# Attention with a spectral mix on one core: the next unit's keys ahead of this unit's queries, loads first, PSUM pools re-dealt, transformed rows mode-innermost, seven weight buffers

## The chip, the cores and the metric

One core of one Trainium2 chip runs the whole program. The metric is device time in microseconds (us) of one execution; lower is better. Each kernel was executed several times on a chip, beside executions of the kernel before on the same chip.

## The reference, cut to what matters

```python
# q, k, v: (8 batches, 8 heads, 576 rows, 64);  w_phi: (64, 128)
def phi(x):
    proj = x @ w_phi                                  # 128 features
    proj = proj - max(abs(proj), axis=-1)             # one value per row
    return concat([exp(proj), exp(-proj)], axis=-1)   # 256 features
kv  = phi(k).T @ v ;  z = sum(phi(k), rows)
x   = (phi(q) @ kv) / (phi(q) @ z)                    # linear attention

X   = rfft(x, axis=rows)[:64]                         # 64 modes kept
Y   = X @ (w_r + 1j * w_i)                            # one 512 x 512 matrix per mode
u   = x + irfft(Y)
out = u + relu(u @ w_ch)
```

The two mode weights are 64 x 512 x 512 numbers each, in float32: 134 MB to be read from memory, converted to bfloat16 on the way.

## The kernel before: the parts that matter

The work is cut into 16 *units*: a unit `(g, bp)` is a pair of heads `g` (4 of them) and a pair of batches `bp` (4 of them). One turn of the main loop, here called a *pass*, handles one unit. Twelve of the passes also carry four *mixes*, the products of transformed rows with the mode weights of the heads before, so there are passes without mixes (the first four) and with them. (Measured from one unit to the next, as in the tables below, that gives four lengths without mixes and ten or eleven with them. The engines are named by their short names: PE multiplies matrices, ACT, DVE and POOL work element by element, SP only issues transfers here.)

PSUM, where the matmuls put their results, is dealt out by two small functions. `one` has four buffers, `two` has two larger ones, and each call takes the next buffer in turn, once its last reader is done:

```python
    ps1 = ctx.enter_context(tc.tile_pool(name="ps1", bufs=4, space=bass.MemoryType.PSUM))
    ps2 = ctx.enter_context(tc.tile_pool(name="ps2", bufs=2, space=bass.MemoryType.PSUM))
    def one(shape, dt=F32):
        return ps1.tile(shape, dt, name="one", tag="one")
    def two(shape, dt=F32):
        return ps2.tile(shape, dt, name="two", tag="two")
```

Which product uses which of them:

```python
    def transposed(src, name):                  # used for k, then for q
        for lo, hi in ((0, 5), (5, 9)):
            ptr = one([128, hi - lo, 128], BF16)          # two halves, in `one`
            for j in range(lo, hi):
                nc.tensor.transpose(ptr[:, j - lo, :], flat[:, j * 128:(j + 1) * 128], ident_b)
            nc.scalar.copy(dst[:, lo:hi, :], ptr)         # and two copies
    # ... absmax(): projects k or q, two products in `two`, the rest in `one`
    def front(st):
        kT = transposed(st["kb"], "kT")
        # ... AB = exp(+-projection of k); ee = exp(-+max); va = v * ee
        qT = transposed(st["qb"], "qT")
        # ... AQ = exp(+-projection of q), the projections in `two`; then absmax of q
    def back(st, XT):
        pk = two([128, 2, 512])                           # the k-v product, in `two`
        # ... 40 matmuls AB x va; one copy of pk to kvz
        for i in range(2):
            pn = [two([128, 2, 512]) for _ in range(2)]   # the numerator, in `two`
            # ... 16 matmuls AQ x kvz; DVE divides them; result in xs
        # ... px: the transform of xs (in `one`), copied to XT in four pieces
    # main loop
    for n, u in enumerate(units):
        front(st[u])
        # ... issue loads of unit n+2, and of mode weights (pool of 6 buffers)
        back(st.pop(u), XTs[g])
        # ... up to four mixes
    yall = pw.tile([128, B_, DMODEL], BF16, name="yall", tag="wt")  # a weight buffer
    # ... remaining mixes; 128 small transfers gather yst into yall; output stage
```

Of the kernel before, what the change touches and what calls it, by code (L numbers as in the profile page):

```python
# [12 lines left out]
I32 = mybir.dt.int32  # L13
# [15 lines left out]
def kernel(  # L29
# [27 lines left out]
    ident_f = const.tile([128, 128], F32, name="ident_f")  # L57
    make_identity(nc, ident_f)
    ident_b = const.tile([128, 128], BF16, name="ident_b")
    nc.vector.tensor_copy(ident_b, ident_f)  # L60

    w2blk = const.tile([128, 256], BF16, name="w2blk")
    nc.vector.memset(w2blk, 0.0)
    nc.gpsimd.dma_start(w2blk[0:64, 0:128], w_phi)
    nc.gpsimd.dma_start(w2blk[64:128, 128:256], w_phi)
    wchb = const.tile([128, 4, 512], BF16, name="wchb")

    CF = const.tile([128, 6, 4, 64], BF16, name="CF")
    CI = const.tile([128, 5, 128], BF16, name="CI")

    def tables():

        def sc(i):
            return yacc[:, i, 0:320].rearrange("p (c m) -> p c m", c=5)

        sp = const
        si = sp.tile([128, 5], I32, name="si")
        nc.gpsimd.iota(si[:, 0:4], [[1, 4]], base=0, channel_multiplier=4)
        nc.gpsimd.iota(si[0:64, 4:5], [[1, 1]], base=512, channel_multiplier=1)
        nc.gpsimd.iota(si[64:128, 4:5], [[1, 1]], base=512, channel_multiplier=1)  # L80
        mi = sp.tile([128, 64], I32, name="mi")
        nc.gpsimd.iota(mi, [[4, 2], [8, NO], [1, 4]], base=0, channel_multiplier=0)
        sf = sp.tile([128, 5], F32, name="sf")
        nc.vector.tensor_copy(sf, si)
        mf = sp.tile([128, 64], F32, name="mf")
        nc.vector.tensor_copy(mf, mi)
        prodf = sc(0)
        nc.vector.tensor_tensor(
            out=prodf,
            in0=sf.unsqueeze(2).to_broadcast([128, 5, 64]),  # L90
            in1=mf.unsqueeze(1).to_broadcast([128, 5, 64]),
            op=ALU.mult,
        )
        MAGIC = 8388608.0
        uu = sc(1)
        nc.vector.tensor_scalar_mul(out=uu, in0=prodf, scalar1=1.0 / S_)
        nn = sc(2)
        nc.vector.tensor_scalar_add(out=nn, in0=uu, scalar1=MAGIC)
        nc.vector.tensor_scalar_add(out=nn, in0=nn, scalar1=-MAGIC)
        dd = sc(3)  # L100
        nc.vector.tensor_tensor(out=dd, in0=nn, in1=uu, op=ALU.is_gt)
        nc.vector.tensor_tensor(out=nn, in0=nn, in1=dd, op=ALU.subtract)
        r0 = sc(4)
        nc.vector.tensor_scalar_mul(out=dd, in0=nn, scalar1=float(S_))
        nc.vector.tensor_tensor(out=r0, in0=prodf, in1=dd, op=ALU.subtract)
        rs = sc(1)
        nc.vector.tensor_single_scalar(out=dd, in_=r0, scalar=288.0, op=ALU.is_ge)
        nc.vector.tensor_scalar_mul(out=dd, in0=dd, scalar1=-float(S_))
        nc.vector.tensor_tensor(out=rs, in0=r0, in1=dd, op=ALU.add)
        rc = sc(2)  # L110
        nc.vector.tensor_single_scalar(out=dd, in_=r0, scalar=144.0, op=ALU.is_ge)
        nc.vector.tensor_scalar_mul(out=dd, in0=dd, scalar1=-float(S_))
        nc.vector.tensor_scalar_add(out=dd, in0=dd, scalar1=144.0)
        nc.vector.tensor_tensor(out=rc, in0=r0, in1=dd, op=ALU.add)
        W = 2.0 * math.pi / S_
        csf = yacc[:, 5:7, :].rearrange("p a e -> p (a e)")[:, 0:640].rearrange(
            "p (c r m) -> p c r m", c=5, r=2)
        nc.scalar.activation(csf[:, :, 0, :], rc, ACT.Sin, scale=W)
        nc.scalar.activation(csf[:, :, 1, :], rs, ACT.Sin, scale=-W)

        nc.gpsimd.memset(CF[:, 4:6], 0.0)
        for p0, p1, d, n in ((0, 128, 0, 4), (0, 64, 4, 1), (64, 128, 5, 1)):
            src = csf[p0:p1, min(d, 4):min(d, 4) + n]
            dst = CF[p0:p1, d:d + n]
            nc.vector.tensor_copy(dst[:, :, 0:2, :], src)
            nc.vector.tensor_scalar_mul(out=dst[:, :, 2, :], in0=src[:, :, 1, :], scalar1=-1.0)
            nc.vector.tensor_copy(dst[:, :, 3, :], src[:, :, 0, :])
        coef = sp.tile([128, 1], F32, name="coef")
        nc.vector.memset(coef, 2.0 / S_)
        nc.vector.memset(coef[0:1, :], 1.0 / S_)  # L130
        nc.vector.memset(coef[64:65, :], 0.0)
        for c in range(5):
            pct = one([128, 128])
            nc.tensor.transpose(pct, csf[:, c, :, :].rearrange("p r m -> p (r m)"), ident_f)
            nc.vector.tensor_scalar_mul(out=CI[:, c, :], in0=pct, scalar1=coef)


    xs = pers.tile([128, B_, 4, DMODEL], BF16, name="xs")
    xr = pers.tile([128, NP, DMODEL], BF16, name="xr")
    yacc = pers.tile([128, NO, DMODEL], F32, name="yacc")  # L140


    XTb = [pers.tile([128, 2, 32, 8, B_], BF16, name=f"XT{i}") for i in range(2)]
    for x in XTb:
        nc.gpsimd.memset(x, 0.0)

    pw_cm = tc.tile_pool(name="pw", bufs=6)
# [7 lines left out]
    def load(g, bp):  # L155
        qb = pin.tile([128, 18, D_], BF16, name="qb")
        kb = pin.tile([128, 18, D_], BF16, name="kb")
        vn = pin.tile([128, 18, D_], F32, name="vn")
        for t, src, eng in ((kb, k, nc.gpsimd), (qb, q, nc.gpsimd), (vn, v, nc.sync)):
            for i in range(2):  # L160
                b = 2 * bp + i
                hs = src[b, 2 * g:2 * g + 2]
                eng.dma_start(  # L163
                    t[:, 8 * i:8 * i + 8, :].rearrange("p (h c) d -> p h (c d)", h=2),
                    hs[:, 0:512, :].rearrange("h (p c) d -> p h (c d)", c=4),
                )
                eng.dma_start(
                    t[64 * i:64 * i + 64, 16:18, :],
                    hs[:, 512:576, :].rearrange("h p d -> p h d"),
                )  # L170
        return dict(g=g, bp=bp, qb=qb, kb=kb, vn=vn)

    def transposed(src, name):

        dst = pm.tile([128, 9, 128], BF16, name=name, tag="xT", bufs=3)
        flat = src.rearrange("p n d -> p (n d)")
        for lo, hi in ((0, 5), (5, 9)):
            ptr = one([128, hi - lo, 128], BF16)
            for j in range(lo, hi):
                nc.tensor.transpose(ptr[:, j - lo, :], flat[:, j * 128:(j + 1) * 128], ident_b)  # L180
            nc.scalar.copy(dst[:, lo:hi, :], ptr)  # L181
        return dst

    def absmax(tT, m):

        for i in range(2):
            ps = two([128, 8, 128])
            for j in range(4):
                nc.tensor.matmul(  # L189
                    ps[:, 2 * j:2 * j + 2, :].rearrange("p c f -> p (c f)"),  # L190
                    lhsT=tT[:, 4 * i + j, :], rhs=w2blk, start=True, stop=True,
                )
# [334 lines left out]
```

## Time and profile before

The kernel before takes 664.12 us (median of 4 runs, 663.99 to 664.2); the profiled run has a span of 661.9 us.

| stretch | us | what sets it |
|---|---|---|
| start to the first transposes of k | 0 to 31.2 | table work ahead of it on PE |
| passes without mixes | 27.0 each (25.7 the first) | a chain through PE, ACT and DVE |
| passes with four mixes | 27.8 to 30.7 each | the same chain, and mixes |
| gather of the mixed rows | 502.4 to 590.3 | 128 transfer issues on SP |
| output stage | 590.3 to 661.9 | PE |

The first fence is from the page of the kernel before: the span, the busy time of each engine with its share, then three rows with 40 slices of the span (the granted clock of PE in tenths, the busy share of the transfer engines, and GB/s).

```profile
span 661.9 us, 7649 instructions
PE 373.7 (56%) x2938; PEld 212.3 (32%) x2957; DVE 281.7 (43%) x452; ACT 252.3 (38%) x432; POOL 209.6 (32%) x288
PEclk9999565565856666665857668575775555559999
GB/s 111 157 189 207 39 49 40 56 36 37 167 181 205 151 210 145 215 141 212 154 186 207 171 216 168 209 183 101 206 104 208 210 210 201 31 10 0 144 144 285
PE 36%; ACT 32%; SPq 12%; DVE 10%; POOL 3%; issue 3%; DMA 2%; another core or an unknown queue 0%; DVEq 0%; ACTq 0%; POOLq 0%
```

No engine is full. The last line is the chain that ended last: the time goes to PE and ACT in turn, 36% and 32%. That is what a serial chain looks like.

The next two fences show one pass without mixes, as the timeline of ACT and then of PE tells it. Columns: start us, duration us, engine, line of the kernel, operation, written tile and read tiles, shapes, count, and in brackets how long the engine sat idle just before and what ended that.

```profile
96.27 3.77 ACT L240 ACTIVATE AQ<-two 128x1024 bf16<-128x1024 f32 x4 [0.61 <-remote]
105.03 0.59 ACT L275 CAST kvz<-two 128x520 bf16<-128x520 f32 x1 [2.41 <-PE two L271]
111.07 1.18 ACT L181 COPY kT<-one 128x640 bf16<-128x640 bf16 x2 [5.45 <-PE one L180]
```

```profile
100.09 1.01 PE L189 MATMUL two<-w2blk,qT 128*128 128x256 bf16 x4 [0.82 <-ACT AQ L240]
100.90 0.43 PE L266 MATMUL two<-va,AB 128*128 128x65 bf16 x4
105.67 1.04 PE L287 MATMUL two<-kvz,AQ 128*128 128x65 bf16 x16 [0.68 <-ACT kvz L275]
109.42 1.03 PE L336 MATMUL one<-CF,xs 128*128 128x256 bf16 x4 [0.44 <-DVE xs L303]
110.24 0.84 PE L180 MATMUL one<-ident_b,kb 128*128 128x128 bf16 x6
```

Read them together. The last projections of q (100.09) wait until the exponentials AQ have emptied a buffer of `two`. Only then come the k-v product (100.90), its copy `kvz` (105.03), the numerator (105.67 to 109), the transform (109.42) and, last of all, the transposes of the *next* k (110.24). ACT sits idle for 5.45 us until those are done. From the first AQ to the copy of the next kT, 14.80 us pass (96.27 to 111.07), with nothing of the next unit under way.

The start, on PE:

```profile
29.38 1.09 PE L134 MATMUL one<-ident_f,yacc 128*128 128x128 f32 x4 [29.38 <-ACT yacc L118]
31.18 1.17 PE L180 MATMUL one<-ident_b,kb 128*128 128x128 bf16 x9
```

The gather, listed by its tile (durations min, median, max in ns, first and last start):

```profile
L393 SPq DMA_DIRECT2D yall<-yst x128: 634/635/800, 502.4 to 589.7; - x128
```

### The profile page before, as it was taken

The numbers are of one execution on the slowest core, as the hardware profiler recorded it, in microseconds if no ns is written. First come the engines' busy times: TensorE is split into PE (matmuls) and PEld (weight loads), VectorE is DVE, ScalarE is ACT, GpSimd is POOL, SyncE is SP. The second block draws the span as 40 slices with busy tenths as digits, with TensorE's granted clock in tenths as the row PEclk, the third lists the DMA queues.
The fourth block names the chain that finished last, engine by engine and source line by source line (L and its number), as shares of the span: only waits on it lengthen the run. The fifth ranks groups of instructions, "written<-read, shape, count | busy, mean of one in ns | idle before, by whom it ended". The sixth has DMA issues, their size and how long they took to land.

```text
span 661.9 us, 7649 instructions
## 1 busy us (share of the span) xinstructions
PE 373.7 (56%) x2938; PEld 212.3 (32%) x2957; DVE 281.7 (43%) x452; ACT 252.3 (38%) x432; POOL 209.6 (32%) x288
## 2 busy tenths in 40 slices
PE   0155658457484767566585755858552222027896
PEld 0134436244243444334243432424320000003442
DVE  0644546345344343455545445544440000017755
ACT  0164472753827263634618265372610000004330
POOL 9653041230534333333535434342143220000000
PEclk9999565565856666665857668575775555559999
DMA  6999132331999999999999999996969999100337
GB/s 111 157 189 207 39 49 40 56 36 37 167 181 205 151 210 145 215 141 212 154 186 207 171 216 168 209 183 101 206 104 208 210 210 201 31 10 0 144 144 285
DMA packets 112084, 97.54 MB, mean 147 GB/s; under 512 B 18864, under 2 KB 110512, under 8 KB 111024
## 3 DMA queue, kind: packets, MB, share of 16 engines
q0 software_dynamic: 94896, 77.12, 74.8%
q1 hardware_dynamic: 17152, 19.93, 10.0%
q8 instruction: 23, 0.38, 0.2%
q14 instruction: 13, 0.11, 0.0%
HBM read 163.64 MB, written 9.44 MB: 261 GB/s over the span
## 4 chain that ended last, share of the span: by engine, by line
PE 36%; ACT 32%; SPq 12%; DVE 10%; POOL 3%; issue 3%; DMA 2%; another core or an unknown queue 0%; DVEq 0%; ACTq 0%; POOLq 0%
SPq L393 12%; ACT AQ L240 9%; PE two L266 6%; PE two L189 6%; PE one L372 6%; ACT AB L214 5%; ACT AB L213 5%; PE one L473 5%; PE one L336 4%; PE two L271 3%; ACT qT L181 3%; DVE ub L456 3%; PE two L287 3%; ACT XT_84 L346 2%; ACT XT_85 L346 2%
## 5 line engine op out<-in xcount | busy, mean ns | idle before, releaser
L356 POOL DMA_DIRECT2D wt<-in_moe_w_r_dram x64 | 49.3, 770 | 91.7 <-PE one L372 71.7
L233 PE MATMUL two<-qT,w2blk 128*128 128x512 bf16 x49 | 24.5, 571 | 87.6 <-ACT qT L181 56.9
L221 DVE TENSOR_TENSOR va<-vn,ee 128x1152 bf16<-128x1152 f32 x32 | 42.3, 1365 | 68.0 <-ACT ee L216 68.0
L465 ACT COPY uT<-one 128x512 bf16<-128x512 bf16 x36 | 18.3, 620 | 132.3 <-DVE ub L456 110.7
L372 PE MATMUL one<-wt,XT_85 128*32 128x512 bf16 x256 | 33.6, 561 | 59.8 <-DMA wt<-in_moe_w_i_dram 30.7
L240 ACT ACTIVATE AQ<-two 128x1024 bf16<-128x1024 f32 x64 | 61.3, 1090 | 2.4 <-remote 2.4
L193 DVE TENSOR_REDUCE mk<-two 128x8 f32<-128x1024 f32 x32 | 37.7, 1220 | 54.1 <-PE two L189 54.1
L356 POOL DMA_DIRECT2D wt<-in_moe_w_i_dram x64 | 49.5, 774 | 17.5 <-DMA wt<-in_moe_w_i_dram 16.7
L266 PE MATMUL two<-va,AB 128*128 128x65 bf16 x512 | 51.9, 244 | 0.0
L193 DVE TENSOR_REDUCE mq<-two 128x8 f32<-128x1024 f32 x32 | 39.2, 1225 | 21.2 <-PE two L189 21.2
L287 PE MATMUL two<-kvz,AQ 128*128 128x65 bf16 x512 | 35.8, 241 | 22.0 <-ACT kvz L275 10.9
L219 POOL CAST va<-ee 128x36 bf16<-128x36 f32 x16 | 21.1, 1317 | 81.8 <-issue 79.8
L189 PE MATMUL two<-w2blk,qT 128*128 128x256 bf16 x128 | 32.4, 407 | 21.0 <-ACT AQ L240 21.0
L163 POOL DMA_DIRECT2D kb<-in_k_dram x32 | 23.4, 731 | 63.7 <-PE one L180 63.7
L287 PEld LDWEIGHTS <-AQ 128*128 128x128 bf16 x512 | 32.1, 128 | 24.8 <-issue 22.8
L189 PE MATMUL two<-w2blk,kT 128*128 128x256 bf16 x128 | 24.1, 352 | 23.9 <-ACT kT L181 23.8
L233 PEld LDWEIGHTS <-w2blk 128*128 128x128 bf16 x64 | 7.3, 114 | 94.3 <-issue 93.4
L346 ACT CAST XT_84<-one 128x128 bf16<-128x128 f32 x32 | 19.6, 991 | 46.8 <-PE one L340 46.8
L387 DVE TENSOR_TENSOR yst<-one,yacc 128x512 bf16<-128x512 f32 x8 | 5.5, 692 | 74.5 <-DMA yall<-yst 63.0
L163 POOL DMA_DIRECT2D qb<-in_q_dram x32 | 23.6, 738 | 40.8 <-DMA wt<-in_moe_w_r_dram 30.6
L266 PEld LDWEIGHTS <-AB 128*128 128x128 bf16 x512 | 33.4, 124 | 9.2
L346 ACT CAST XT_85<-one 128x128 bf16<-128x128 f32 x32 | 19.6, 993 | 40.3 <-PE one L340 40.3
(152 smaller groups left out, 748.8 us busy)
## 6 DMA issues: line engine op xcount, KB each, us to landing
wt<-in_moe_w_r_dram POOLq DMA_DIRECT2D x64, 512.0 KB, 12.7
wt<-in_moe_w_i_dram POOLq DMA_DIRECT2D x64, 512.0 KB, 14.5
vn<-in_v_dram SPq DMA_DIRECT2D x32, 256.0 KB
out_dram<-of SPq DMA_DIRECT2D x8, 1024.0 KB
kb<-in_k_dram POOLq DMA_DIRECT2D x32, 128.0 KB, 10.9
qb<-in_q_dram POOLq DMA_DIRECT2D x32, 128.0 KB, 6.3
yall<-yst SPq DMA_DIRECT2D x128, 8.0 KB
vn<-in_v_dram SPq DMA_DIRECT2D x32, 32.0 KB
```

Source lines behind the costliest of these rows:

```text
L163: eng.dma_start(t[:, 8 * i:8 * i + 8, :].rearrange("p (h c) d -> p h (c d)", h=2), hs[:, 0:512, :].rearrange("h (p c) d -> p h (c d)", c=4),)
L189: nc.tensor.matmul(ps[:, 2 * j:2 * j + 2, :].rearrange("p c f -> p (c f)"), lhsT=tT[:, 4 * i + j, :], rhs=w2blk, start=True, stop=True,)
L193: nc.vector.tensor_reduce(out=m[:, 8 * i:8 * i + 8], in_=ps, axis=AX.X, op=ALU.max, apply_absolute_value=True,)
L213: nc.scalar.activation(AB[:, 0, sl, :], ps, ACT.Exp, scale=1.0)
L221: nc.vector.tensor_tensor(out=va[:, ab, :, 0:64], in0=st["vn"], in1=ee[:, ab, :].unsqueeze(2).to_broadcast([128, 18, 64]), op=ALU.mult,)
L240: nc.scalar.activation(AQ[:, ab, i], ps, ACT.Exp, scale=1.0 - 2.0 * ab)
L266: nc.tensor.matmul(o, lhsT=AB[:, ab, n, :], rhs=va[:, ab, n, :], start=(c == 0), stop=False,)
L287: nc.tensor.matmul(pn[ab][:, h, c * 65:(c + 1) * 65], lhsT=AQ[:, ab, i, c % 2, 2 * h + c // 2, :], rhs=kvz[:, i, h, ab, :], start=True, st ...
L346: nc.scalar.copy(XT[:, t, :, :, 2 * bp + i] .rearrange("p m (u w x) -> p w u x m", u=2, w=2)[:, t], px[:, i, :, 32 * t:32 * t + 32].rearra ...
L356: nc.gpsimd.dma_start(wt[:, i], w[mg * MG:(mg + 1) * MG, g * 128:(g + 1) * 128, :].rearrange("m p e -> p m e"),)
L372: nc.tensor.matmul(py[32 * j:32 * j + 32, :], lhsT=XT[:, t, 4 * o + j, 4 * i:4 * i + 4, :].rearrange("p r b -> p (r b)"), rhs=wt[:, i, j, ...
L393: nc.sync.dma_start(yall[n:n + 1, :, :], yst[r:r + 8, :])
```

## The change

The stated intent: run the keys of the next unit beside the queries of this one; put the loads at the head of the program; keep transformed rows with the mode innermost; have seven weight buffers in place of six. The diff also deals the PSUM pools anew. Its core (cuts marked `...`; renamed helpers, a different order of heads and rows within `xs`, and table arithmetic with fewer instructions are left out):

```diff
-    pw_cm = tc.tile_pool(name="pw", bufs=6)
+    XTb = [pers.tile([128, 10, B_, NMODES], BF16, name=f"XT{i}") for i in range(2)]
+    pw_cm = tc.tile_pool(name="pw", bufs=7)
...
+    st = {(0, 0): load(0, 0)}            # ahead of identity and tables
...
     def transposed(src, name):
-        for lo, hi in ((0, 5), (5, 9)):
-            ptr = one([128, hi - lo, 128], BF16)
-            ...
-            nc.scalar.copy(dst[:, lo:hi, :], ptr)
+        ptr = two([128, 9, 128], BF16)
+        for j in range(9):
+            nc.tensor.transpose(ptr[:, j, :], flat[:, j * 128:(j + 1) * 128], ident_b)
+        nc.scalar.copy(dst, ptr)
...
+    def keys(st):                        # k's transposes, projections, exponentials, va
+        ...
+        for i in range(2):
+            pk = one([128, 4, 65])       # the k-v product belongs to the keys now
+            ...
+            nc.scalar.copy(kvz[:, i], pk)
+    def queries(st, XT):                 # q's, then the numerator and the transform
+        ...
+        for n0 in (0, 6, 12):
+            pn = [one([128, 6, 65]) for _ in range(2)]
...
-            pn = [two([128, 2, 512]) for _ in range(2)]
...
+        nc.scalar.copy(XT[:, 2:10, 2 * bp:2 * bp + 2, :]...)   # one copy, was four
...
     for n, u in enumerate(units):
-        front(st[u])
+        ...
+        if n + 1 < len(units):
+            keys(st[units[n + 1]])
+        if n == 0:
+            tables()
-        back(st.pop(u), XTs[g])
+        queries(st.pop(u), XTb[g % 2])
...
-    yall = pw.tile([128, B_, DMODEL], BF16, name="yall", tag="wt")
+    yall = XTb[0]...                     # no longer in a weight buffer
```

## The prediction

> **What bounds the kernel now.** No engine is full: the page gives PE 56%, DVE 43%, ACT 38% of 661.9 us. The chain of waits shows four stretches.
> 1. Start, 0-31 us. First transposes of k run at 31 us, though k, issued at 9.3-12, lands in 3.4 us. Two POOL memsets of 3.5 us go before the loads, and the table arithmetic on DVE before the unit.
> 2. Five units without mix, 27.0 us apart (the chain repeats at 57.8, 84.8, 111.8). PE is busy 16.6, ACT 14.2, DVE 13.1 us of each (busy by window): a serial chain.
> 3. Eleven units with four mixes, 28.4-30.7 us apart, mean 29.2; clock 0.58-0.65. DMA doesn't bind: 4.19 MB of weights at 209 GB/s (weights-only stretch 496-530) is 20 us; with q, k, v I estimate 25.6.
> 4. Tail. The 128 gather issues on the SP queue take 87.9 us (0.69 each), 502.4 to 590.3. They wait 9.5 us for a buffer, because yall sits in a weight buffer. Then 71.6 us of output stage.
>
> **What the change does.**
> - Start: k is issued at about 1.7 us and the table arithmetic is shorter. First transposes at 9 us.
> - Overlap: keys of the next unit stand before queries of this one. But the changed kernel's order puts, on ACT, both kvz copies of the next unit before the four AQ exponentials of this one, and on PE all its kv matmuls before the query projections. The Trainium skill ("TensorE: Matmul & The Clock Gate", engine queue depths) says ACT and DVE are strict FIFO and PE pulls only weight loads ahead. So much of the overlap is lost: one pass is k copy, projection, absmax, 6 exponentials, va (2.6), kv (4), kvz, 4 AQ exponentials, numerator, next transposes. With the trace's durations (exponentials 0.92 apart, reductions 1.2, kv matmuls 0.1 each) I get 25.0 us without mixes, where it was 27.0.
> - Mix passes: PE's order now puts the 32 mix and 7 px matmuls between the first two projections of k and the rest, on the chain. A group of four mixes takes 0.43 us at the low clock. I get 28.2 us (half warm) to 30.2 (cold): at best one less than now.
> - Fewer ACT instructions: XT 4x0.6 us becomes one, one copy per transposed tensor, one ee. Mostly off the chain.
> - Seventh weight buffer: little. yall in XTb[0] removes the 9.5 us wait.
>
> **Sum.** Unit 2's transposes copied at 45 us (now 83.5); first mix at 148 (now 164); ten mix passes at 28.6; a short last unit of 17: its mixes at 448 (now 485). First gather at 457, 88 us of gather, 1.3, 71.6 of output: 618 us. The gain is head start (16 us at the first mix), gather (10) and the shorter last unit (12); little is steady state.
>
> **What would show it.** First k transposes at 8-11 us; mix passes 27.5-30 us apart; ACT idle before kvz, then AQ; gather starting within 3 us of the first yst and still 88 us; output stage unchanged.
>
> **What would make it wrong.** A warmer PE clock, or real overlap, gives passes near DMA's 25.6 us and about 590 us; then weights would be waited for. Mode-innermost XT makes weight loads of 32 strided columns: if slower, mixes lengthen. The order may cost more than estimated (31 us a pass gives 640).
>
> Predicted 620 us, 8 in 10 between 596 and 643; faster by over 2%: 0.93, within 2%: 0.06, slower: 0.01.

## The result, and the profile after

The changed kernel takes 565.98 us (median of 4 runs, 560.55 to 566.7) against 664.12 us. The ratio is 0.8505, with a 95% interval of 0.8452 to 0.8557. Ratios in this document are the mean time of one kernel's runs over the mean of the other's runs of the same rounds, so they are not quite the ratios of the medians quoted. Executions over 1.5% slower than the fastest of the same kernel are left out of the means. A second set of 6 runs on another chip gave 564.73 us (one of the six was slow; the five fast ones have a median of 563.84) and 0.8524 (0.8491 to 0.8556).

| stretch | before | predicted | after |
|---|---|---|---|
| first transposes of k | 31.2 | 9 | 8.4 |
| pass without mixes | 27.0 (25.7 the first) | 25.0 | 19.8 to 20.2 (21.9 the first) |
| pass with mixes | 27.8 to 30.7 | 28.6 (of 27.5 to 30) | 22.5 to 26.9 (24.7 on average) |
| first mix at | 164.4 | 148 | 127.1 |
| gather | 502.4 to 590.3 | 457, then 88 long | 403.3 to 491.2 |
| output stage | 71.6 | 71.6 | 72.9 |
| total | 664.1 | 620 | 566.0 |

(The length of a pass is taken from one start of the first activation that writes `ee` to the next.) The same lines of the page as before:

```profile
span 564.1 us, 7674 instructions
PE 344.4 (61%) x2957; PEld 207.1 (37%) x2957; DVE 287.6 (51%) x481; ACT 223.7 (40%) x351; POOL 186.9 (33%) x273
PEclk9997876957879586685758785786655555579899
GB/s 162 99 210 196 214 167 77 31 64 170 214 186 208 192 200 197 217 199 205 204 204 206 204 206 204 204 207 206 207 210 210 209 210 134 12 0 66 103 243 260
PE 33%; DMA 18%; ACT 17%; SPq 14%; DVE 9%; issue 5%; POOL 3%; DVEq 0%; POOLq 0%; ACTq 0%
```

Two things stand out. ACT's share of the chain fell from 32% to 17%, and DMA's rose from 2% to 18%: from about the middle of the span the GB/s row stands flat at 204 to 210. The change has moved the kernel against its memory traffic.

One pass without mixes again, ACT and then PE:

```profile
92.14 0.29 ACT L208 ACTIVATE ee<-mk 128x36 f32<-128x36 f32 x1
98.06 0.38 ACT L233 CAST kvz<-one 128x260 bf16<-128x260 f32 x1 [0.56 <-PE one L229]
99.69 1.94 ACT L256 ACTIVATE AQ<-two 128x1024 bf16<-128x1024 f32 x2 [0.16 <-PE two L249]
101.62 1.94 ACT L256 ACTIVATE AQ<-two 128x1024 bf16<-128x1024 f32 x2
103.43 1.14 ACT L166 COPY kT<-two 128x1152 bf16<-128x1152 bf16 x1
```

```profile
94.32 0.42 PE L223 MATMUL one<-va,AB 128*128 128x65 bf16 x4
101.68 0.66 PE L276 MATMUL one<-kvz,AQ 128*128 128x65 bf16 x16 [1.60 <-ACT AQ L256]
102.18 0.50 PE L165 MATMUL two<-ident_b,kb 128*128 128x128 bf16 x6
102.70 0.29 PE L276 MATMUL one<-kvz,AQ 128*128 128x65 bf16 x4
102.83 0.33 PE L165 MATMUL two<-ident_b,kb 128*128 128x128 bf16 x3
```

The order that the prediction saw is there: both `kvz` copies stand before the AQ exponentials on ACT. But look at 102.18 and 102.83. The transposes of the next k run *between* the numerator's matmuls, while ACT still computes exponentials, and ACT copies their result at 103.43 without a moment idle. From the first AQ to the copy of the next kT it is 3.74 us (99.69 to 103.43), where it was 14.80. The two stretches do not hold the same work: in the kernel before, the k-v product and its copy lie between the two as well. A like comparison is from the first matmul of the numerator to the next transposes: 0.50 us here (101.68 to 102.18) against 4.57 before (105.67 to 110.24).

The start and the gather:

```profile
8.43 1.12 PE L165 MATMUL two<-ident_b,kb 128*128 128x128 bf16 x9 [8.43 <-DVE ident_b L105]
```

```profile
L358 SPq DMA_DIRECT2D XT_69<-yst x128: 634/635/792, 403.3 to 490.6; - x128
```

The gather starts 99 us earlier and is as long as it was (87.9 us), and the output stage nearly so. Everything that was gained was gained before it.

### The profile page after: what moved, and what is told of

It reads as the page before. It is cut to its first block, busy times and chain, and to the rows that moved or that the text cites. A ratio compares the mean times of both kernels' runs of the same rounds, so it can differ in the third digit from the quotient of the medians.

```text
span 564.1 us, 7674 instructions
## 1 busy us (share of the span) xinstructions
PE 344.4 (61%) x2957; PEld 207.1 (37%) x2957; DVE 287.6 (51%) x481; ACT 223.7 (40%) x351; POOL 186.9 (33%) x273
## 4 chain that ended last, share of the span: by engine, by line
PE 33%; DMA 18%; ACT 17%; SPq 14%; DVE 9%; issue 5%; POOL 3%; DVEq 0%; POOLq 0%; ACTq 0%
SPq L358 14%; DMA wt<-in_moe_w_i_dram 14%; PE two L179 6%; PE one L448 6%; PE one L223 6%; ACT AQ L256 5%; ACT AB L204 4%; DMA qb<-in_q_dram 3%; DVE mk L182 3%; PE one L229 3%; DVE ub L428 3%; PE one L337 3%; ACT AB L205 3%; ACT qT L166 2%; PE one L305 2%
## 5 line engine op out<-in xcount | busy, mean ns | idle before, releaser
L276 PE MATMUL one<-kvz,AQ 128*128 128x65 bf16 x512 | 34.4, 222 | 25.7 <-ACT AQ L256 25.4
L223 PE MATMUL one<-va,AB 128*128 128x65 bf16 x512 | 48.6, 232 | 0.0
L79 POOL DMA_DIRECT2D kb<-in_k_dram x32 | 23.3, 728 | 63.9 <-DMA wt<-in_moe_w_r_dram 24.8
L204 ACT ACTIVATE AB<-two 128x1024 bf16<-128x1024 f32 x32 | 32.9, 1027 | 26.1 <-DVE mk L182 26.1
L276 PEld LDWEIGHTS <-AQ 128*128 128x128 bf16 x512 | 26.6, 116 | 40.5 <-ACT AQ L256 39.0
L337 PEld LDWEIGHTS <-XT_70 128*32 128x32 bf16 x256 | 11.1, 160 | 82.3 <-issue 63.0
L165 PE MATMUL two<-ident_b,qb 128*128 128x128 bf16 x144 | 14.0, 249 | 35.4 <-ACT AB L205 35.4
L305 PE MATMUL one<-CF,xs 128*128 128x256 bf16 x160 | 30.0, 310 | 5.0 <-DVE xs L296 4.8
L205 ACT ACTIVATE AB<-two 128x1024 bf16<-128x1024 f32 x32 | 33.0, 1030 | 0.0
L451 DVE SCALAR_TENSOR_TENSOR of<-one,ub 128x512 f32<-128x512 f32 x36 | 24.9, 692 | 15.7 <-PE one L448 15.7
```

Source lines behind the costliest of these rows:

```text
L79: eng.dma_start(t[:, 8 * i:8 * i + 8, :].rearrange("p (h c) d -> p h (c d)", h=2), hs[:, 0:512, :].rearrange("h (p c) d -> p h (c d)", c=4),)
L204: nc.scalar.activation(dst[:, 0], ps, ACT.Exp, scale=1.0)
L205: nc.scalar.activation(dst[:, 1], ps, ACT.Exp, scale=-1.0)
L223: nc.tensor.matmul(o, lhsT=ABs[i][:, ab, 4 * h + c, :], rhs=va[:, ab, 8 * i + 4 * h + c, :], start=(c == 0), stop=False,)
L276: nc.tensor.matmul(pn[ab][:, n - n0, :], lhsT=AQs[i][:, ab, c % 2, 2 * h + c // 2, :], rhs=kvz[:, i, 2 * h + ab, :], start=True, stop=True,)
L337: nc.tensor.matmul(py[32 * j:32 * j + 32, :], lhsT=XT[:, s0:s0 + 4, :, 32 * t + 4 * o + j].rearrange("p r b -> p (r b)"), rhs=wt[:, i, j, ...
```

## The experiments

Fifteen runs. The main theory at the start was that the pass became shorter because keys of the next unit overlap with queries of this one. The first rival was that it became shorter for reasons that have nothing to do with which unit the keys belong to, above all the PSUM pool in which each product lives. Each edit is on the changed kernel unless a line says otherwise, and ratios are to the kernel before. Differences in us between kernels of different calls are differences of medians, on different chips, and good to a few us.

### Keys of the same unit

```diff
-    keys(st[units[0]])
...
-        if n + 1 < len(units):
-            keys(st[units[n + 1]])
+        keys(st[u])
```

> The changed kernel, but each pass does the keys and the queries of the same unit (keys no longer run a unit ahead). Theory A (mine, from the instruction order of this kernel): the scheduler puts the instructions of a pass in the same order as in the changed kernel, and in both the key-value product of a pass stands before its query exponentials, so a pass without mixes stays at 20 us (20 to 21); the first mix comes a key chain earlier (about 113 us instead of 127), and since later passes are bound by the weight DMA the total falls to 548-558 us. Rival B (the intent of the change): running keys beside queries of the previous unit is what shortens the pass; without it a pass without mixes goes back towards 25-27 us and the total to 595 us or more.

Measured: 559.97 us (one of the four runs was slow; 559.79 for the three fast ones), ratio 0.8409 (0.8357 to 0.8461), some 6 us *faster* than the changed kernel. The intervals of the two ratios just touch (0.8452 to 0.8557); against the changed kernel's second set (0.8491 to 0.8556) they are apart. Its passes without mixes are 19.8 to 20.4 us, the same. The first mix comes at 114.8 us instead of 127.1. The scheduler pulls the next k's transposes between the numerator's matmuls anyway, so running a unit ahead in the program text buys no overlap, and only delays the first queries. The idea in the change's own description is not what shortened the pass.

### The numerator back in `two`

```diff
-            pn = [one([128, 6, 65]) for _ in range(2)]
+            pn = [two([128, 6, 65]) for _ in range(2)]
```

> The changed kernel with the numerator products again in the two-bank PSUM pool that transposes and projections use (as in the kernel before; there are two such buffers). Theory A: a good part of the shorter pass comes from freeing this pool, so that the next unit's transposes go into the middle of the numerator; here they come after it, and a pass without mixes takes 22.5-25 us, the first mix comes at 137 us or later, the total is 575-590 us. Rival B (the gain is the overlap of keys and queries): at most 1 us a pass, the total within 5 us of the changed kernel's 566.

Measured: 608.57 us, ratio 0.9162 (0.9127 to 0.9196). The effect is 43 us, well above what was expected. Passes without mixes are 23.9 to 25.3 us. The timeline of this run (PE, then ACT) shows why:

```profile
91.26 0.49 PE L276 MATMUL two<-kvz,AQ 128*128 128x65 bf16 x6 [0.72 <-DVE nd L289]
94.79 0.32 PE L284 MATMUL two<-kvz,AQr 128*64 128x65 bf16 x4
95.18 1.12 PE L165 MATMUL two<-ident_b,kb 128*128 128x128 bf16 x9
96.39 1.12 ACT L166 COPY kT<-two 128x1152 bf16<-128x1152 bf16 x1 [4.49 <-PE two L165]
```

The numerator takes three pairs from a pool of two buffers, so each pair waits for DVE to read the one before, and the k transposes, which need a buffer of the same pool, come after all of it (95.18, behind the last numerator matmul at 94.79). They start at 95.18, just after DVE has read the first tile of the last pair (94.57 to 95.13). ACT is idle for 4.49 us. That is most of the 5.1 us by which the pass is longer. Nothing in the arithmetic or in the order of the program text was changed.

### The transposes back in halves in `one`

```diff
-        ptr = two([128, 9, 128], BF16)
-        ...
-        nc.scalar.copy(dst, ptr)
+        for lo, hi in ((0, 5), (5, 9)):
+            ptr = one([128, hi - lo, 128], BF16)
+            ...
+            nc.scalar.copy(dst[:, lo:hi, :], ptr)
```

> The changed kernel with the transposes in two halves in the one-bank pool, with two copies, as in the kernel before; all else as changed. If the halved transposes make most of the 41 us that the numerator's pool leaves open, passes are 22 to 24 us and the total 590 to 605 us. If they matter only when the two-bank pool is crowded, passes stay at 20 to 21 us and the total at 563 to 572 us.

Measured: 620.91 us, ratio 0.9352 (0.932 to 0.9383), 55 us slower than the changed kernel: more than either theory allowed for. Passes without mixes are 24.8 to 27.7 us. PE, then ACT:

```profile
89.18 0.71 PE L166 MATMUL one<-ident_b,qb 128*128 128x128 bf16 x5
92.72 0.61 PE L166 MATMUL one<-ident_b,qb 128*128 128x128 bf16 x4
89.99 0.69 ACT L167 COPY qT<-one 128x640 bf16<-128x640 bf16 x1 [3.50 <-PE one L166]
103.22 1.18 ACT L167 COPY kT<-one 128x640 bf16<-128x640 bf16 x2 [2.89 <-PE one L166]
```

Now the transposes share `one` with the k-v product and the numerator, and stand in the middle of the first (89.18, 92.72) and behind the second. ACT waits 3.50 and 2.89 us for them. The two stretches of the pass that grow are from `ee` to the first AQ, 10.26 us against 7.55, and from the first AQ to the kT copy, 6.77 against 3.74. (The edit changes the pool and the number of copies together; no run separates the two.)

### Numerator and k-v product both in `two`

```diff
-            pk = one([128, 4, 65])
+            pk = two([128, 4, 65])
...
-            pn = [one([128, 6, 65]) for _ in range(2)]
+            pn = [two([128, 6, 65]) for _ in range(2)]
```

> The changed kernel with both the numerator and the k-v product in the two-bank pool. With the numerator alone there the pass was 25.3 us and the total 608.6 us. If the k-v product's pool makes most of the rest of the way to 650, this has passes of 26.5 to 27.5 us and a total of 628 to 645 us. If the pool of the k-v product does not matter and the halved transposes do, it stays at 25 to 25.5 us and 605 to 613 us.

Measured: 672.71 us, ratio 1.0153 (1.0113 to 1.0193): all of the gain is gone, and more. The total was expected at most at 645. Passes without mixes are 28.4 to 28.7 us. The transposes of q now stand behind the whole k-v product in the queue of PE, and their copy on ACT comes after both `kvz` copies, at 98.17:

```profile
96.94 1.14 PE L165 MATMUL two<-ident_b,qb 128*128 128x128 bf16 x9
98.17 1.12 ACT L166 COPY qT<-two 128x1152 bf16<-128x1152 bf16 x1 [0.76 <-PE two L165]
```

### Pools and layout as they were

The numerator and the k-v product in `two`, transposes in halves in `one`, and the old layout of the transformed rows with four copies; the order, the loads and the seven buffers stay.

```diff
+        for lo, hi in ((0, 5), (5, 9)): ptr = one(...) ...; nc.scalar.copy(...)
+            pk = two([128, 4, 65])
+            pn = [two([128, 6, 65]) for _ in range(2)]
+    XTb = [pers.tile([128, 2, 32, 8, B_], BF16, name=f"XT{i}") for i in range(2)]
+    ... four copies of px
```

> The changed kernel with its numerator and its k-v product back in the two-bank pool that the queries' products also use, and with the old layout of the transformed rows (two half transposes, four copies). If which PSUM pool a product uses, with the count of copies, is what shortens the pass, the unmixed pass goes back to 26 to 28 us and the total to 620 to 645 us. If it is the order of emission (overlap) that shortens it, the unmixed pass stays at or below 25 us and the total below 610 us.

Measured: 649.75 us, ratio 0.9798 (0.977 to 0.9825), passes without mixes 27.3 to 27.4 us. The pass went all the way back to the 27.0 us of the kernel before, as the pool theory said (26 to 28); the total came out slightly above its range of 620 to 645. On the same chip the changed kernel took 564.73 us. So 85 of the 99 us gained go with these parts. The parts don't add: with the transposes in halves this is 23 us *faster* than the run above, whose transposes were whole.

### The new pools alone in the kernel before

The old order of emission, the old layout, six buffers, tables first:

```diff
 # on the kernel before
-            ptr = one([128, hi - lo, 128], BF16)          # two halves
+        ptr = two([128, 9, 128], BF16)                    # whole, one copy
-        pk = two([128, 2, 512])
+            pk = one([128, 4, 65])                        # per batch
-            pn = [two([128, 2, 512]) for _ in range(2)]
+                pn = [one([128, 4, 65]) for _ in range(2)]  # per batch and head
```

> The kernel before, in its own order of emission, with only the pools changed: transposes whole in the two-bank pool with one copy, the k-v product in two one-bank tiles and the numerator in one-bank tiles. If the pools are what shortens the pass, whatever the order, unmixed passes fall from 27.0 to 20 to 23 us and the total to 570 to 610 us. If the pools need the new order of emission, where the k-v product precedes the queries' exponentials, passes stay at 25 us or more and the total at 630 us or more.

Measured: 595.4 us, ratio 0.8997 (0.8948 to 0.9046). This is the strongest run: 68 of the 98 us come with the pools alone, in the old order of emission. "The pools" here means also what goes with them: one copy of the transposes in place of two, the k-v product in two tiles, the numerator in four pairs of smaller tiles. Passes without mixes are 20.5 to 21.7 us, but for one of 24.5. On PE the k transposes now run before or among the numerator's matmuls in the passes without mixes, as in the changed kernel (PE, then ACT, of this run; then its start on PE). In its passes with mixes they still come behind the transform, and these passes are 25.4 us on average, against 29.3 before and 24.7 in the changed kernel. So the place of the transposes is not all that the pools changed:

```profile
108.66 0.43 PE L286 MATMUL one<-kvz,AQ 128*128 128x65 bf16 x4
108.89 1.04 PE L179 MATMUL two<-ident_b,kb 128*128 128x128 bf16 x8
109.73 0.87 PE L286 MATMUL one<-kvz,AQ 128*128 128x65 bf16 x12
110.03 1.12 ACT L180 COPY kT<-two 128x1152 bf16<-128x1152 bf16 x1 [1.52 <-PE two L179]
```

```profile
12.44 0.61 PE L179 MATMUL two<-ident_b,kb 128*128 128x128 bf16 x4 [12.44 <-DMA kb<-in_k_dram]
```

The second fence is a surprise. The first k transposes moved from 31.18 to 12.44 us, with the tables and memsets where they had been. In the kernel before, those transposes followed the table's own transposes, which are in `one` too and waited for a table value until 29.38; in `two` they are not behind them. So a good part of the late start was also the pool, and not only the memsets and the table arithmetic that the prediction named.

### The old layout of transformed rows

The array has the batch innermost again, and four copies write it. (Edit: the XT lines of the run above, alone.)

> The changed kernel with the transformed rows in the old layout (modes outside, four 0.6 us copies a unit on ACT instead of one; weight loads of the mix of 32 adjacent columns instead of 32 strided ones). If the copies stand on the chain of a pass (on ACT they come before the key exponentials of the rest): a pass without mixes 1 to 2 us longer, passes with mixes too as long as they are not bound by DMA; the total 8-14 us longer (574-580). If they are off the chain: within 3 us of 566. Strided weight loads: if they cost anything, the mix bursts (22 matmuls in 1.54 us in the changed kernel) get shorter here.

Measured: 575.19 us, ratio 0.8664 (0.8637 to 0.8691), 9 us slower than the changed kernel. Passes without mixes are 22.0 to 22.7 us: three more ACT instructions, in front of the exponentials of k, lengthen the chain. The prediction feared that mode-innermost rows would make the weight loads of the mixes slower. They are slower each (160 to 165 ns on average for the loads of 32 columns, 101 ns here), but an undisturbed burst of 22 mixes takes 1.54 us there against 1.47 here, so it costs less than a tenth of a microsecond per burst.

### Six weight buffers

```diff
-    pw_cm = tc.tile_pool(name="pw", bufs=7)
+    pw_cm = tc.tile_pool(name="pw", bufs=6)
```

> The changed kernel with six weight buffers instead of seven. Prediction's view (DMA does not bind): within 3 us. Theory A after the result (from about unit 7 on the passes are bound by the weight DMA at 205 GB/s and the seventh buffer holds one tile of 5 us more at the first mix): 3 to 8 us longer (569-574), because one tile less is loaded before the first mix; in the DMA-bound passes themselves no change.

Measured: 573.69 us, ratio 0.8652 (0.861 to 0.8694), 8 us slower. My expectation missed where: the passes without mixes stay at 20.2 us, and the late passes, which I had thought fixed by the traffic itself, grow to 27.2 to 28.5 us from 24.6 to 26.9. With one buffer less the transfers move 199 GB/s from 221 to 360 us of the span, against 205.

### Tables and memsets first

```diff
-    st = {(0, 0): load(0, 0)}            # from before the identity and tables
+    ... # memsets of XTb whole, then tables()
+    st = {units[0]: load(*units[0]), units[1]: load(*units[1])}
+    keys(st[units[0]])
```

> The changed kernel with the old start: both buffers of transformed rows zeroed whole on POOL, and the tables written, before the first loads of k and q. Theory: the lead of the loads is worth what the first pass is delayed by: the first transposes of k run at 16-24 us instead of 8.4, the first mix moves by the same 8-15 us, later passes are unchanged, total 573-582 us (against 566 for the changed kernel and 560 without the unit ahead). Rival: the weight DMA, not the compute chain, sets the end, so that a late start is hidden: within 3 us of 566.

Measured: 570.62 us, ratio 0.8603 (0.8574 to 0.8632). The first transposes came 9.6 us later (18.0), but the total rose by only 4.6 us, less than expected (573 to 582): the first mix is 5.8 us later, the gather 3.7 us, so later stretches absorb the rest. One line is worth a look, as DVE and then POOL show it:

```profile
2.87 3.24 DVE L106 CAST w2blk<-wpf 64x128 bf16<-64x128 f32 x1 [1.25 <-DMA wpf<-in_w_phi_dram]
6.14 4.53 DVE L107 CAST w2blk<-wpf 64x128 bf16<-64x128 f32 x1
1.67 4.37 POOL L371 MEMSET XT<- 128x5120 bf16 x1
6.23 4.37 POOL L371 MEMSET XT<- 128x5120 bf16 x1
```

A small cast that takes 0.22 and 0.34 us in the changed kernel takes 3.24 and 4.53 us here, ending when the POOL memset beside it ends. The Trainium skill ("SBUF — State Buffer", Who interferes with whom) says that a cast on DVE in a two-port mode and GpSimd contend for a shared port pair and that the later one is blocked for the whole instruction. The durations agree with that, though no view shows in which mode the casts ran. The second cast began slightly before its memset by the trace (6.14 and 6.23), which by itself doesn't fit the order that the page gives, but spans on POOL are rough.

### Half of the weights

Only the real weights are loaded, and used twice. The result is wrong; the comparison with the reference is not sensitive to this part of the sum.

```diff
-        for i, w in ((0, moe_w_r), (1, moe_w_i)):
+        for i, w in ((0, moe_w_r),):
...
-                    rhs=wt[:, i, j, :], ...
+                    rhs=wt[:, 0, j, :], ...
```

> The changed kernel with only the real half of each weight tile loaded, and used in place of the imaginary half too (wrong results on purpose, half the weight bytes, all instructions of the engines as before). Theory A (late passes are bound by the weight DMA): passes with mixes stay at 22.5-24 us to the end instead of 24.5-27, the gather starts at 380-392 us instead of 403, the gather itself still takes 88 us (it is bound by its 128 issues of 0.69 us), total 543-555 us. Rival, the view of the prediction (DMA does not bind): within 4 us of 566.

Measured: 548.51 us (two runs, one round), ratio 0.827 (0.8223 to 0.8316). The gather begins at 387.4 us, 16 us earlier. So half of the weight traffic costs the changed kernel about 17 us, nearly all after its eighth unit. Busy times by window (window, its length, five engines with counts, granted clock, transfer share, GB/s) for late passes, first of the kernel before, then the changed one, then this run:

```profile
300.00:440.00 140.00, 91.90 (x815) 53.66 (x819) 71.76 (x110) 68.40 (x118) 62.21 (x85) 0.66 1.16 188
```

```profile
221.00:360.00 139.00, 94.37 (x879) 60.38 (x876) 79.31 (x134) 67.75 (x104) 56.87 (x81) 0.72 1.25 205
```

```profile
221.00:340.00 119.00, 82.37 (x813) 52.98 (x812) 71.76 (x119) 60.85 (x95) 38.65 (x56) 0.75 0.83 132
```

### The gather's target out of a weight buffer, in the kernel before

```diff
 # on the kernel before
-    yall = pw.tile([128, B_, DMODEL], BF16, name="yall", tag="wt")
+    yall = XTb[0].rearrange("p t m r b -> p (t m r b)").rearrange("p (b e) -> p b e", b=B_)
```

> The kernel before with one part of the change: the gathered rows go into the idle buffer of transformed rows and no longer into a weight buffer. Expected: the gather starts within 3 us of the first sum (493 us instead of 502.4), and the total is 8 to 11 us shorter: 653-656 us. Rival: the end of the gather is set by the arrival of the weights, so it starts earlier and ends as before: within 2 us of 664.

Measured: 655.79 us, ratio 0.9888 (0.9861 to 0.9915). As expected: the gather starts at 494.0 instead of 502.35 us. This step of the prediction (9.5 us) was right to about a microsecond.

### The k-v product in the other order

```diff
             for h in range(2):
-                for ab in range(2):
+                for ab in (1, 0):
```

> The changed kernel with the two halves of the k-v product in the other order, so that its first ten matmuls need the second of the two v writes. If starting the k-v product on the first v half alone is part of why the pass came out shorter than predicted, the unmixed pass grows by 1 to 1.4 us to 21.2 to 21.6 and the total is 570 to 575 us. If the product waits for both halves anyway, the pass stays 20.2 us and the total 562 to 568 us.

Measured: 568.51 us, ratio 0.8569 (0.8546 to 0.8592). DVE writes `va` in two halves, one after the other, 2.63 us for both. In the changed kernel the first ten matmuls of the k-v product need only the first half, and start at 94.32 while DVE is at the second (92.64 to 95.27). Here they need the second. The passes without mixes are 20.9 to 22.0 us, 21.5 on average; those of the changed kernel on the same chip are 19.8 to 21.6, 20.6 on average. That looks like what the theory said, but the clock gives another reading. In the changed kernel the stretch from `ee` to the first AQ takes 7.4 to 7.6 us in some passes and 8.5 to 8.6 in others; here it is 8.4 in all but the first and one other. Windows over this stretch (columns as under "Half of the weights"; the granted clock is the third figure from the end), first one pass of this run, then two of the changed kernel on the same chip:

```profile
50.70:59.10 8.40, 6.88 (x53) 4.55 (x55) 5.50 (x6) 2.01 (x6) 4.18 (x7) 0.50 1.29 209
```

```profile
70.20:78.70 8.50, 6.96 (x53) 4.74 (x55) 5.50 (x6) 2.67 (x7) 3.76 (x7) 0.50 1.27 211
91.80:99.20 7.40, 6.01 (x53) 4.25 (x55) 5.50 (x6) 2.69 (x8) 2.18 (x4) 0.68 0.69 120
```

At a clock of 0.50 the changed kernel is no faster in this stretch than this run (8.56 us against 8.44); it is faster only where the clock rises within the stretch. So the run does not show that the early start on the first half is worth anything by itself. Whether the order of the halves is what holds the clock down here (0.688 to 0.699 over the whole span in its four runs, 0.729 to 0.749 in the fast runs of the changed kernel on this chip) is not shown. The total grew by about 4 us, less than expected (570 to 575; 564.73 for the changed kernel on the same chip): the first mix is 4.4 us later than in the changed kernel's run there, and later passes, bound by transfers, give some of it back.

### Two queues for the gather, with keys of the same unit

```diff
 # on the run with keys of the same unit
-                        nc.sync.dma_start(yall[n:n + 1, :, :], yst[r:r + 8, :])
+                        eng = nc.sync if (t + i) % 2 == 0 else nc.scalar
+                        eng.dma_start(yall[n:n + 1, :, :], yst[r:r + 8, :])
```

> Candidate to beat both: keys and queries of the same unit in a pass, and the 128 gather issues shared between the SP and the ACT queue (ACT is idle then). If the tail is bound by the issues of one queue, the gather then ends about 7 us after the last sum, which waits for the last weights: 5 to 9 us off the 560 us of the run with only the first of the two: 551-556 us. If it is bound by something else in the tail: 560.

Measured: 552.27 us, ratio 0.8342 (0.8296 to 0.8387). Two queues halve the issue time each has to bear, yet the gather still takes 83.0 us instead of 87.9. What holds it now is the arrival of the weights, as PE and then DVE show it for the last sum:

```profile
468.95 0.66 PE L337 MATMUL one<-wt,XT 128*32 128x512 bf16 x4 [1.93 <-DMA wt<-in_moe_w_i_dram]
469.66 0.69 DVE L352 TENSOR_TENSOR yst<-one,yacc 128x512 bf16<-128x512 f32 x1 [10.42 <-PE one L337]
```

The eight sums come about 11 us apart, each within 0.05 us of the end of its last matmul, and that matmul waits for weights, which move at 210 GB/s (400 to 460 us). The gather ends 6 us after the last sum (470.4 to 476.5), where it is 12 us in the changed kernel (478.8 to 491.2). The list of waits puts five of the eight sums down to the landing of earlier transfers of the gather (51.6 us in all), but as these sums too start at the end of their matmul, the landing did not hold them.

The Trainium skill ("Trainium Kernel Development and Optimization", Key Constraints) says that transfers issued from several engines run on the same 16 engines and save only the issue time. This run fits it: 5 us saved of 88, though 64 of the 128 issues left SP.

### Three buffers for the gathered sums

```diff
 # on the run before
-            yst = pm.tile([128, DMODEL], BF16, name="yst")
+            yst = pm.tile([128, DMODEL], BF16, name="yst", bufs=3)
```

> The same-unit kernel whose gathers are issued from two queues, with three instead of two buffers for the gathered sums. If the sums wait for gathers to land only because there are two buffers, the total is 547 to 551 us. If the landing itself bounds that stretch, it stays at 552 us, within 0.5%.

Measured: 554.87 us, ratio 0.836 (0.8336 to 0.8385), from 5 rounds. No gain: the gather still takes 82.9 us (398.50 to 481.38), and the last mixes still wait for weights. So more buffers don't help, as was to be expected where the weights set the pace. Held against the changed kernel on the same chip (next run), this version is some 2% faster, with intervals that don't overlap.

### The changed kernel again

> The changed kernel, unaltered, on the same chip as the three above: 560 to 568 us, with unmixed passes of 20.2 us. It is the reference that the others are held against.

Measured: 564.73 us, ratio 0.8524 (0.8491 to 0.8556), from 5 rounds; passes without mixes 19.8 to 21.6 us.

### What the runs say together

The two stretches of a pass without mixes that the pools decide, from the timelines (us):

| kernel | `ee` to first AQ | first AQ to next kT copy | pass | total |
|---|---|---|---|---|
| changed kernel | 7.55 | 3.74 | 20.2 | 566 |
| numerator in `two` | 8.5 | 8.4 | 25.3 | 609 |
| transposes in halves in `one` | 10.3 | 6.8 | 24.8 to 27.7 | 621 |
| numerator and k-v product in `two` | 12.0 | 8.1 | 28.4 to 28.7 | 673 |
| pools and layout as before | 9.6 | 7.3 | 27.4 | 650 |

(The first two columns are of one pass each. The passes of one kernel differ with the clock: in the changed kernel's later passes the first stretch is 7.3 to 8.6 us. The pools act at equal clock too: at a mean of 0.58 the changed kernel's pass is 21.6 us, in its second set, and at 0.57 that with the numerator in `two` is 25.3.)

Where the next k transposes stand on PE goes with the pools in all seventeen traces. With the transposes in `two` and the numerator in `one` they stand before the transform, within the numerator, in every pass of the changed kernel and of the runs that keep its pools. With both in `two` they come after the numerator. With the transposes in `one`, which the transform uses as well, they come after the transform's first matmuls; that is the case of the kernel before, where numerator and transposes are *not* in the same pool. Only the run with the new pools in the kernel before is divided: before or among the numerator in the passes without mixes, behind the transform in those with them. How the order on PE's queue is chosen when the program is built, no run shows.

The gain of 98 us, told from the new pools put into the kernel before: 68 us are the pools, with the tiles and copies that go with them, and with the part of the earlier start that they brought. The remaining 30 us match the sum of what the other parts cost when taken away singly: 9 (layout and copies), 8 (seventh buffer), 8 (the gather's target, measured on the kernel before), 5 (start), which is 30. That this sum fits is partly luck, since the parts interact, and the keys a unit ahead, which by themselves *cost* about 6 us, would have to be taken off it.

A version faster than both: keys of the same unit, with the gather on two queues, 552.27 us, 17% less than before.

## Why the prediction was wrong

It said 620 us, between 596 and 643, and 0.93 for faster by over 2%. The direction was right. The time was 54 us less than predicted, and outside the range.

What held, point by point:

- The start. "First transposes at 9 us" was 8.4. The reason given, earlier loads and shorter table work, is only part of it: the new pools alone gave 12.4, so the number was in part luck.
- The order on ACT: both `kvz` copies before the AQ exponentials, with ACT idle for 3.4 us before AQr and again before `kvz`; seen in the timeline.
- The tail. The gather is still 88 us, it starts within about a microsecond of the first sum, and the output stage is nearly unchanged (72.9 us against 71.6). That the gather's target frees 9.5 us was measured at 8.
- The failure that the prediction itself named, passes near the 25.6 us of the transfers and weights waited for, is what came: the late passes are 24.6 to 26.9 us.

The step that failed is "I get 25.0 us without mixes, where it was 27.0", and with it "28.2 us (half warm) to 30.2 (cold)" for passes with mixes and "little is steady state". The prediction counted one pass as a chain that ends in "4 AQ exponentials, numerator, next transposes", one after the other. The trace shows another path: the next transposes run between the numerator's matmuls (102.18) while ACT is still at the exponentials, and ACT goes from the last of these to the copy of kT without idle time (103.43). The pass is 20.2 us, and the ten mixed ones are 24.7 on average against 28.6. Where the numerator was put back in `two`, numerator and transposes do stand one after the other at the end, ACT waits 4.49 us for them, and the pass is 23.9 to 25.3 us, about what the prediction had. So the overlap that it left out is the one that the pools make.

How its own sum divides is less clear. The text gives few of its terms. The later split of the 25.0, which can't be checked, stands here against the trace of one pass:

| part of the pass | summed before | measured |
|---|---|---|
| copy of kT to first projection of k | 2.9 | 1.96 |
| to the first exponential of k | 2.5 | 2.36 |
| to `ee` | 5.1 | 4.64 |
| to the first AQ exponential | 10.1 | 7.55 |
| to the copy of the next kT | 4.4 | 3.74 |
| sum | 25.0 | 20.25 |

By this split most of the miss lies before the first AQ, and little at the end, which doesn't go well with the reading above. How the 4.8 us divide therefore stays open. Three candidates, of different standing:

1. *The pools.* The prediction looked at what each engine does in what order and counted fewer copies. It never asked which pool each product takes its buffers from, and what goes before it there. With the numerator, the transposes or the k-v product in another pool, in the four arrangements tried, the pass is 24 to 29 us, about as long as the prediction had thought it or longer. That the pools decide the pass is shown, by taking them away (85 us with the layout) and by adding them alone (68 us). That this is all of the missing piece of the sum is not.
2. *The clock.* The prediction took k-v matmuls at 0.1 us each. In the pass shown, four of them take 0.40 us at 97.12 and 0.30 at 97.59, and windows read a clock of 0.50 from 95.6 to 97.4 and 1.00 from 97.5 to 99.6. The Trainium skill ("TensorE: Matmul & The Clock Gate", Part 1) says that the clock is released by sustained activity, in two states. The trace agrees. In the second set one pass has a clock of 0.50 from `ee` past the next kT copy, and takes 21.6 us; its neighbours take 19.8 and 20.2. So the warmer clock is worth some 1.5 us of the 4.8, and at the low clock the pass is still 3.4 us shorter than predicted. In the mixed passes the granted clock is 0.72 after against 0.66 before, in the windows shown above; there a warmer clock is as much an effect of the shorter pass as its cause, and no run separates the two.
3. *The halves of `va`.* The prediction counted `va` (2.6) and then the k-v product (4), one after the other. The product starts on the first half of `va` 0.95 us before the second is written. But the run with the other order is no slower in this stretch at the same clock (8.44 us against 8.56), so that this shortens the pass is not shown.

Two smaller steps were wrong as well. "DMA doesn't bind" is false after the change: 17 us, by the run with half the weights. (For the kernel before it was not tested.) "Seventh weight buffer: little" was 8 us, as one buffer more keeps the transfers busier (205 against 199 GB/s). And the gain of the headline idea, keys beside queries, for which the prediction lost "much of the overlap" but not all, is about -6 us (some 1%).

Why the pass depends so much on the pools can in part be read in the lines. The Trainium skill ("TensorE: Matmul & The Clock Gate", Engine queue depths), quoted in the prediction, says that ACT and DVE are strictly first-in first-out, and the traces agree: a `kT` copy that waits 4.49 us for its transposes holds up everything behind it on ACT. In that run the transposes start when DVE has read a tile of their pool. In the kernel before no such wait is seen: the transposes stand right behind the transform in PE's queue (110.24, no idle time before them). The Trainium skill ("Perfetto Trace Analysis", Optimization Strategy) says of a gap that repeats through a stretch on one engine that it "can mean there isn't enough SBUF/PSUM for the next tile to be allocated". The 5.4 us of ACT's idle time before each kT copy, in the passes without mixes of the kernel before, may be such a gap; with the new pools alone it is 1.4 to 2.5 us. Prediction and profile had this clue in plain sight: PE wrote the transposes right behind the transform, with nothing of its own to wait for.

## What to carry to other kernels

Where a pass is a serial chain and no engine is full, ask of every product not only which engine runs it and in what order, but which pool it takes its PSUM buffer from, and who else takes buffers from that pool before it: moving the numerator out of the pool of the transposes, one word in the source, is worth 43 us here. Test a headline idea alone: here the visible reordering cost about 6 us, while a re-dealing of pools that the description left out was worth most of the gain. And after a large gain ask again what binds: transfers that "don't bind" at 29 us a pass do at 24.

## What the Trainium skill lacked or had wrong

- "Perfetto Trace Analysis" (Matmuls; Optimization Strategy) says to rotate matmul groups through different PSUM banks and that a repeating gap can mean too little PSUM, but it gives no size, and says nothing of *which* products should share a pool. Here a pool shared by the numerator and the transposes costs 43 us of 566, and a bad split of the same PSUM makes it 673 us. It also doesn't say that a one-time product at the start (the table transposes) can hold up the first unit through a shared pool: 31.2 against 12.4 us.
- "TensorE: Matmul & The Clock Gate" (Part 1) gives the clock as two states. Agreed: the clock records of all seventeen traces hold only 0.50 and 1.00, so the means of 0.56 to 0.75 over longer stretches are mixtures of the two.
- "Trainium Kernel Development and Optimization" (Key Constraints) says that several issuing engines only save issue time. Nothing here goes against it: 64 of 128 issues moved to a second queue took 5 us off 88, and the 83 us that stay are set by weights still arriving.
- "SBUF — State Buffer" (Who interferes with whom) says that a blocked cast waits for the whole of the other instruction. Agreed: 0.22 to 0.34 us became 3.24 and 4.53 us beside a POOL memset of 4.37 us. The order that the page gives for who blocks whom could not be confirmed for the second one.
